# A Fourier-plus-experts kernel: the second group's key matrix gets its own space, five staged blocks move behind the first evictions, and token 512's row is normalized later

## The chip, the cores and the metric

The kernel runs on one core of a Trainium2 chip. The metric is device time in microseconds (us) from launch to the end of the program, and lower is better. Five engines work side by side, each through its own queue in order: TensorE (PE: matmuls, with PEld for its weight loads), VectorE (DVE), ScalarE (ACT), GpSimd (POOL) and SyncE (SP), whose queue issues nearly all the DMAs. An engine that reaches an instruction whose inputs are not there stands still, with everything behind it.

## The reference

The input `x` has 2048 tokens of 512 numbers. The output is the sum of three things:

```
xn = layernorm(x)
A  = C_seq.re @ (xn @ C_hid.re.T) - C_seq.im @ (xn @ C_hid.im.T)   # real part of a 2-D DFT
q  = xn @ w_q                       # 32 heads, two halves of 128
s1, s2 = q1 @ k1.T, q2 @ k2.T       # 64 first keys, 64 second keys
two best of each -> two best of the four pairs -> experts e, gates g = softmax
B  = sum over heads and experts of g * gelu(xn . u[e]) * v[e]
out = x + A + B
```

## The kernel before, in words

All the work that the change touches lies in the first tenth of the run. A planner (the framework's scheduler) simulates the program with its own costs and writes a fixed order for each engine's queue; where two instructions are ready in its simulation, the one earlier in the program goes first. The author steers it by adding dependencies that compute nothing: a column of zeros in the tile `zs` is made from a late result (`scale=0.0`) and given as `bias` to instructions that shall not be queued before that result.

**Normalization and folds.** The tokens lie in four groups g of four blocks of 128 (`x[q, g]`), handled in the order `G = (1, 0, 2, 3)`. `ln(g, n)` (from L335) takes the means and variances, for some blocks on ACT and for the rest on DVE, and then scales the four blocks in place: on ACT (L379), or on DVE through `norm` (L313), which before is used only for the first group (`n == 0`) and its blocks 0 and 2. `fold(k, g)` (L402 to L413) adds (k = 0) or subtracts (k = 1, "difference") mirrored rows and columns on DVE, through the tiles `ft`, `ff`, `fo` into `Q[k][g]`; with that the DFT over the sequence needs a quarter of the matmuls. `main(k, g)` (L433) multiplies `Q[k][g]` by a quarter of the DFT matrix, `A[k, g]`, which `load(k, g)` (L320) brought in as a tile `c`; the sums over g build up in four PSUM banks `p`. `evict(k)` (L499 to L503) copies these four banks to SBUF on ACT (L494, L497), and they are the same four banks that the next user of the tag `pa` needs: `main(1, 0)` after `evict(0)`. `spread()` (L423) makes a correction column `s5c` that half of `evict(0)` adds.

**Token 512's row.** One token that has no mirror image, `x5` (a single partition of 2 x 512), is normalized on ACT (L576), and then folded by `fold_row(0)` and `fold_row(1)` on POOL (L415 to L419, and L390 to L400 with POOL as the engine).

**Staged blocks.** `stage(i)` (L507 to L514) splits a normalized block into two 16-bit parts, a high part on ACT (L512) and the difference on DVE (L513), in one of eight staging places (the table `SB`, L505), and a transposing DMA on SP (L514) writes it to `xt[i]`, the operand of the score matmuls. Sixteen blocks are staged, the n-th of them being `TO[n]`. A staging place is used again by a later block only after the transposing DMA has read it.

**Keys.** Heads are handled in eight groups j of four. `m_mul(j, t, ...)` multiplies the query weights by the keys on PE (L142), and `m_parts(j)` (L224 to L229) splits the four resulting banks into two 16-bit parts: the high one on ACT (L227), the difference on DVE (L228). The result `m` is the moving operand of the score matmuls `s_mm` (L253), 12 for each block. For j = 0 and 2, 4, 6 it lies in the pool `MP[0]`; for odd j in `MP[1]`, which before is opened after `stA.close()` (L677), in the space that the tiles of the pool `da` leave.

**Early scores.** `early(n)` (L278) computes the first group's scores for the n-th staged block ahead of time and parks them in SBUF (L285): before, four of them at the first group's stage, n = 4 and 5 in front of `main(1, 1)`, n = 6 and 7 in front of `main(1, 3)`. Then `m_mul(1)` and `main(1, 3)` follow, and after them on PE the scores of n = 8 to 15. `sides()` (L457) and `sums`, `hid` (L516) finish single rows and columns of the DFT. In `part_b`, `scores` finds the two best keys of each head on DVE (MAX8, L862; FIND_INDEX8, L866). A copy of a corner of `m1` into the place of the best values (L922) holds that row of instructions back until the second keys are split.

**The rest of the run** computes scores for the other groups, then the experts' matmuls (`u_part` L997, `g_mm` L1035, `v_part` L1080); none of it is edited, except for where some single rows are kept.

**Buffers.** The tiles `raw` (4 KB a partition each) hold eight DFT quarters and the four tiles of the first query weights; ten of them exist before. `cst` is a pool that lives through the whole kernel.

Of the kernel before, what the change touches and what calls it, by code (L numbers as in the profile page):

```python
# [7 lines left out]
F32 = mybir.dt.float32  # L8
# [10 lines left out]
P = 128  # L19
# [15 lines left out]
def tile_fnet_peer(ctx, tc, x, ca, cb, c5, wt, wf, wr, wq, kt, ut, vn, out):  # L35
# [90 lines left out]
    MP = {}  # L126
# [128 lines left out]
                n += 1  # L255


    MP[0] = stS.enter_context(tc.tile_pool(name="mp0", bufs=1, side="left"))
    stE = ctx.enter_context(ExitStack())
    uvp = stE.enter_context(tc.tile_pool(name="uvp", bufs=1, side="right"))  # L260
    cmp_p = stE.enter_context(tc.tile_pool(name="cmpp", bufs=1, side="right"))
# [29 lines left out]
        xp[h] = da.tile([P, 2, 512], F32, name=f"x{h}")  # L291

    def raw_tile(name):
        return da.tile([P, 2, 512], F32, tag="raw", name=name, bufs=10)

    G = (1, 0, 2, 3)
    GK = G, (0, 1, 2, 3)
# [33 lines left out]
    zs = da.tile([P, 3], F32, name="zs")  # L331

    def ln(g, n):


        onact = {1: (0, 1), 3: (0,)}.get(n, ())
        for q in onact:
            junk = Q[1][g].rearrange("p a d -> p (a d)").bitcast(BF16)[:, 2:514]
            zero = 0.0
            if n == 3:  # L340

                zero = nm0[:, 0, 0:1]
                nc.scalar.activation(zero, xn(G[1], 3)[:, 0:1], AF.Copy, scale=0.0)
            nc.scalar.activation(junk, xn(g, q), AF.Identity, bias=zero, scale=1.0 / 512, accum_out=mvs[:, g, q, 0:1])
            nc.scalar.activation(junk, xn(g, q), AF.Square, bias=mvs[:, g, q, 0:1], scale=-1.0,
                                 accum_out=mvs[:, g, q, 1:2])
        if onact:
            v = mvs[:, g, 0:len(onact), 1]
            nc.scalar.activation(v, v, AF.Copy, scale=1.0 / 512)
        for q in range(4):  # L350
            if q in onact:
                continue
            if n == 0:
                st = da.tile([P, 6], F32, tag="st", name=f"st{g}_{q}", bufs=2)
            else:
# [11 lines left out]
        nc.vector.scalar_tensor_tensor(negm[:, g], mvs[:, g, :, 0], -1.0, rstd[:, g], op0=ALU.mult, op1=ALU.mult)  # L367
        if g == 0:
            nc.vector.tensor_scalar(nm0[:, 0], negm[:, 0, 2:4], not0, None, op0=ALU.mult)
            nc.vector.tensor_scalar(nm0[:, 1], rstd[:, 0, 2:4], not0, None, op0=ALU.mult)  # L370
        for q in (0, 2, 1, 3):
            t = xn(g, q)
            b, r = negm[:, g, q:q + 1], rstd[:, g, q:q + 1]
            if g == 0 and q > 1:
                b, r = nm0[:, 0, q - 2:q - 1], nm0[:, 1, q - 2:q - 1]
            if n == 0 and q % 2 == 0:
                norm(t, t, 4 * g + q)
            else:
                nc.scalar.activation(t, t, AF.Identity, bias=b, scale=r)  # L379
# [100 lines left out]
        nc.vector.tensor_tensor(a5[0:1, 0], a5[0:1, 0], r[:, 1, 0:257], op=ALU.add)  # L480

    PT = {}
    p256 = uf[12][:, 0:16].rearrange("p (n a) -> p n a", n=8)
    p5 = uf[13][:, 257:263]
    q5 = uf[13][0:1, 0:2]
    s256, a256 = [uf[i].rearrange("p (h t) -> p h t", h=2) for i in (0, 2)]
    a5 = uf[1][:, 0:514].rearrange("p (k d) -> p k d", k=2)

# [18 lines left out]
    def stage(i):  # L507

        src = xn(i // 4, i % 4)
        n = TO.index(i)  # L510
        t = u_sb[SB[n] // 2][:, SB[n] % 2].rearrange("p a k n -> p a (k n)")
        nc.scalar.activation(t[:, 0], src, AF.Identity, bias=zs[:, int(n > 3):int(n > 3) + 1])  # L512
        nc.vector.tensor_tensor(t[:, 1], src, t[:, 0], op=ALU.subtract)  # L513
        nc.sync.dma_start_transpose(xt[i].rearrange("p a k n -> p (a k) n"), t.rearrange("p a d -> p (a d)"))  # L514

# [30 lines left out]
    row512(0, c5r, nc.scalar)  # L546
    nc.gpsimd.tensor_copy(c52, c5r[:, 0:2])
    nc.scalar.dma_start(c55, cb[0, 0, 0, 0:1, 8, 0:1])
    for g in GK[1][:2]:
        load(1, g)  # L550
    wfs = uf[14][:, 0:512]
    for t in range(2):
        m_mul(0, t, (0, 1))
    for n, g in enumerate(G):
# [16 lines left out]
        if n == 1:  # L571
            nc.scalar.activation(zs[:, 0:1], xn(g, 3)[:, 0:1], AF.Copy, scale=0.0)
            for q in range(4):
                stage(4 * G[0] + q)
            for q in range(2):
                nc.scalar.activation(x5[:, q], x5[:, q], AF.Identity, bias=negm[0:1, 0, q + 2:q + 3],  # L576
                                     scale=rstd[0:1, 0, q + 2:q + 3])
            for h in GK[1][2:]:
                load(1, h)
            nc.sync.dma_start(wfs, wf)  # L580
            nc.sync.dma_start(w2, wr[:, 0:2].to_broadcast([P, 2]))
            row512(1, A[1, 0][0:1, 512:1024])
            m_load(1, lambda t: wq_view(t, w4), range(4))
        if n == 3:
            nc.scalar.activation(zs[:, 1:2], rstd[:, G[3], 0:1], AF.Copy, scale=0.0)
            fold_row(0)
            fold_row(1)
            for q in range(2):
                stage(q)
# [14 lines left out]
    for g in GK[1]:  # L604
        fold(1, g)
        if g == 0:
            nc.vector.tensor_copy(Q[1][0][0:1, 0, 1:256], s5i[:, 1:256])
            nc.scalar.activation(xp[1][0:1], x5, AF.Copy)
            for q in range(2, 4):
                stage(q)  # L610
        if g % 2:
            for b in range(3 + g, 5 + g):
                early(b)
        if g == 3:
            for t in range(4):
                m_low(1, t, s5c[:, 0, 0:1])
            for t in range(4):
                m_mul(1, t, range(KD))
        main(1, g)
        if g == 1:  # L620
            for t in range(4):
                m_prep(1, t, whp, s5c[:, 0, 0:1])
# [2 lines left out]
    sides()  # L625
    for q in range(4):
        stage(12 + q)
    evict(1)

    BS = {}  # L630
# [24 lines left out]
    def y_rows(n):  # L655

        if n == 8:
            hid(uf[13][0:1, 264:778], 1, [p5[:, dt:dt + 1] for dt in range(2)], q5,
                [p5[:, 3 + dt:4 + dt] for dt in range(2)], pc("hy5"))
            return  # L660
        g, q = divmod(n, 2)
# [3 lines left out]

    def y_store(n):
        if n == 8:
            t, a, b, r = uf[13][0:1, 264:778], y_d[2][0:1], y_d[3][0:1], slice(0, 1)
        else:
            g, q = divmod(n, 2)  # L670
            r = slice(0 if g else 1, P)
# [3 lines left out]
        nc.sync.dma_start(b[:, 256:512], t[r, 0:256])  # L675

    stA.close()  # L677
    MP[1] = stS.enter_context(tc.tile_pool(name="mp1", bufs=1, side="left"))

# [3 lines left out]
    def part_b(safe, stS, stP, stE, xt, u_sb, cmp_p, w4):  # L683
# [226 lines left out]
        for j in range(NCH):  # L910
# [613 lines left out]
```

## Time and profile before

| | |
|---|---|
| median of the runs, us | 1160.09 (1159.86 to 1160.1, 3 runs) |
| profiled execution, its own time, us | 1157.52 |
| span of that execution in the trace, us | 1155.7 |
| mean granted TensorE clock | 0.993 |
| PE busy | 1128.8 us, 98% of the span |
| DVE busy | 935.7 us, 81% |
| ACT busy | 606.8 us, 53% |
| POOL busy | 223.9 us, 19% |

The span is what the trace covers of the profiled execution; its time has 1.8 us more, around the span. In a timeline, a row gives the start, the length, the engine, the line of the kernel, the operation, the tile written and the tiles read, the shapes, and the number of instructions merged into it; in brackets stands how long the engine had been idle before, and what released it. Matmul ends are modelled, so a long "busy" PE can hide a slow clock; the granted clock of a stretch stands in the view by windows. A transfer's row shows only when SP issued it.

### The profile page before, as it was taken

Reading aid. Unit: us, or ns where it says so; the run is one execution under the profiler, and the core shown is the slowest. Engines: PE = TensorE matmul, PEld = TensorE weight load, DVE = VectorE, ACT = ScalarE, POOL = GpSimd, SP = SyncE. Lnnn points to the kernel's source line nnn. Section 1 sums busy time; section 2 is a strip of 40 time slices with the busy share of each in tenths; the row PEclk is TensorE's granted clock in tenths of the full one; section 3 lists DMA queues with packets and bytes.
Section 4 is the critical chain, followed back from the end, with each engine's and each line's share of the span. In section 5 each row is a group of like instructions: output and inputs, shape, how many; then the busy total and the mean of one; then the engine's idle time right before and its main releaser. Section 6 shows DMA issues by size and latency. Waiting matters only on the chain.

```text
span 1155.7 us, 25202 instructions
## 1 busy us (share of the span) xinstructions
PE 1128.8 (98%) x9866; PEld 719.0 (62%) x9866; DVE 935.7 (81%) x2853; ACT 606.8 (53%) x1045; POOL 223.9 (19%) x216
## 2 busy tenths in 40 slices
PE   5899999999999999999999999999999999999997
PEld 4345555445445459778478478469569559658763
DVE  7879989799898999974995894897886886788670
ACT  6645787687786635353445435535535435334440
POOL 3001474865865410000000000010010000000000
PEclk9999999999999999999999999999999999999999
DMA  9774265143241204261742743743545555452423
GB/s 339 211 201 155 70 205 181 61 160 128 74 165 46 83 15 123 90 210 38 246 158 98 237 160 104 220 165 135 185 159 174 169 173 168 156 166 66 134 77 104
DMA packets 98334, 167.81 MB, mean 145 GB/s; under 512 B 32916, under 2 KB 48155, under 8 KB 98206
## 3 DMA queue, kind: packets, MB, share of 16 engines
q1 hardware_dynamic: 97904, 166.04, 44.5%
q8 instruction: 79, 1.29, 0.5%
q14 instruction: 49, 0.40, 0.1%
q10 hardware_dynamic: 302, 0.08, 0.0%
HBM read 142.69 MB, written 17.63 MB: 139 GB/s over the span
## 4 chain that ended last, share of the span: by engine, by line
PE 89%; DVE 8%; ACT 1%; DMA 1%; issue 0%; DVEq 0%; ACTq 0%
PE z L997 29%; PE v L1080 28%; PE s L253 25%; PE g L1035 4%; PE m L142 2%; DVE u L862 1%; PE p L442 1%; DVE u L866 1%; DVE u L513 1%; DVE ft L409 1%; DVE sums L358 0%; DVE m L228 0%; DVE L L1025 0%; DMA xq<-u 0%; DVE ff L390 0%; DMA x<-in_x_dram 0%
## 5 line engine op out<-in xcount | busy, mean ns | idle before, releaser
L997 PE MATMUL z<-xb,u 128*128 128x256 f16 (+1 forms) x3840 | 342.6, 251 | 0.0
L997 PEld LDWEIGHTS <-u 128*128 128x128 f16 x3840 | 309.7, 98 | 26.4
L253 PE MATMUL s<-m,xq 128*128 128x512 f16 x1344 | 297.6, 379 | 0.0
L1080 PE MATMUL v<-v,act 128*128 128x512 f16 x1056 | 233.2, 379 | 0.0
L253 PEld LDWEIGHTS <-xq 128*128 128x128 f16 x1344 | 129.6, 98 | 151.2 <-issue 1.9
L1025 DVE TENSOR_TENSOR L<-io_lam,cmp 128x2048 f16<-128x2048 f16 x128 | 157.3, 1229 | 60.0 <-PE g L1035 60.0
L1080 PEld LDWEIGHTS <-act 128*128 128x128 f16 x1056 | 101.3, 98 | 117.7
L1093 POOL TENSOR_TENSOR y<-y,xr 128x512 f32<-128x512 f32 x15 | 26.5, 1767 | 612.8 <-DMA y<-y_d 472.7
L862 DVE MAX8 vals<-ss 128x8 f32<-128x64 f32 x896 | 133.7, 216 | 2.6 <-ACT ss L858 2.5
L1004 ACT ACTIVATE act<-z,scl 128x256 f32<-128x256 f32 (+1 forms) x152 | 72.7, 502 | 120.1 <-PE z L997 120.1
L858 ACT ACTIVATE ss<-s,wsc 128x512 f32<-128x512 f32 x120 | 80.6, 682 | 56.3 <-PE s L253 45.7
L1080 PE MATMUL v<-v,w 128*128 128x512 f16 x480 | 106.2, 379 | 0.0
L1156 ACT ACTIVATE cx<-cx 128x896 f32<-128x896 f32 x64 | 60.5, 946 | 70.5 <-DVE cx L1136 52.0
L866 DVE FIND_INDEX8 idx<-vals,ss 128x8 uint16<-128x256 f32 x224 | 93.8, 419 | 0.0
L1050 ACT ACTIVATE act<-w 128x1024 f16<-128x1024 f32 x36 | 48.3, 1358 | 60.0 <-DVE w L1043 59.6
L1080 PEld LDWEIGHTS <-w 128*128 128x128 f16 x480 | 46.1, 98 | 53.3
L1043 DVE SCALAR_TENSOR_TENSOR w<-act,scl,g 128x1024 f32<-128x1024 f32 x44 | 55.7, 1276 | 19.8 <-ACT act L1004 19.8
L1130 DVE TENSOR_TENSOR cx<-cx 128x512 f32<-128x512 f32 (+2 forms) x84 | 48.4, 609 | 26.0 <-DMA cx<-in_cb_dram 24.7
L1035 PEld LDWEIGHTS <-L 128*128 128x128 f16 x2048 | 60.7, 96 | 11.3 <-DVE R L1033 1.3
L1035 PE MATMUL g<-R,L 128*128 128x32 f16 x2048 | 61.9, 176 | 0.3 <-DVE R L1033 0.2
L1033 DVE TENSOR_TENSOR R<-R,cmp 128x512 f16<-128x512 f16 x128 | 60.2, 470 | 1.5
L1004 ACT ACTIVATE w<-z,scl 128x256 f32<-128x256 f32 (+1 forms) x72 | 35.4, 492 | 49.3 <-PE z L997 49.3
(298 smaller groups left out, 1322.8 us busy)
## 6 DMA issues: line engine op xcount, KB each, us to landing
v<-v_d SPq DMA_DIRECT2D x67, 512.0 KB, 5.2
cx<-in_cb_dram SPq DMA_DIRECT2D x64, 448.0 KB, 5.2
w<-in_wq_dram SPq DMA_DIRECT2D x28, 512.0 KB, 5.9
fit<-in_wq_dram SPq DMA_DIRECT2D x28, 512.0 KB, 4.9
uv<-in_vn_dram SPq DMA_DIRECT2D x16, 512.0 KB, 3.8
uv<-in_ut_dram SPq DMA_DIRECT2D x16, 512.0 KB, 3.9
c<-in_ca_dram SPq DMA_DIRECT2D x8, 512.0 KB
y<-y_d SPq DMA_DIRECT2D x16, 256.0 KB, 2.7
```

The source lines that it names most:

```text
L253: nc.tensor.matmul(ps, xt[i][:, l, kd, :], m[:, r, kd, :], start=(n == 0), stop=(n == 3 * KD - 1))
L858: nc.scalar.activation(s, ps, AF.Copy, scale=inv)
L862: nc.vector.max(vals[:, i, w, :, h], s[:, g, :])
L866: nc.vector.max_index(idx[:, i, w].rearrange("p k h -> p (k h)"), vals[:, i, w, 0:2].rearrange("p k h -> p (k h)"), s[:, w * HC:g + 1, :]. ...
L997: nc.tensor.matmul(ps if n == 1 else ps.rearrange("p (b n) -> p b n", b=2), ug[:, l, c % 2, kd, :], xb2[:, k0, r, kd, :] if n == 1 else xb ...
L1004: nc.scalar.activation(ACT[bb][:, cg * m:cg * m + m, :], pv[:, i], AF.Gelu_apprx_tanh, scale=zsc)
L1025: nc.vector.tensor_tensor(L.rearrange("p t (l two) -> p t l two", two=2), io_lam.rearrange("p (l two) -> p l two", two=2).unsqueeze(1).to_ ...
L1033: nc.vector.tensor_tensor(Rv, Rv, bc(2, NC), op=ALU.mult)
L1035: nc.tensor.matmul(p[:, hf, t * NC:(t + 1) * NC], L[:, t, :], R[:, t, :], start=True, stop=True)
L1043: nc.vector.scalar_tensor_tensor(w, act[:, :, ts], fw, p.rearrange("p h (n c) -> p c (h n)", c=NC), op0=ALU.mult, op1=ALU.mult)
L1080: nc.tensor.matmul(pv, w16[:, c, :, l], v_sb[g][:, r, cc, :], start=(n + cc == 0 and k == 0), stop=(n == 15 and cc == 1 and k == 2))
L1156: later.append(lambda: nc.scalar.activation(tf[:, P:], tf[:, P:], AF.Abs, accum_out=chk[:, n:n + 1]))
```

## The change

- **Second keys.** `MP[1]` is opened beside `MP[0]`, ahead of the pool `da`, so that it has space of its own. The tiles `raw` go from ten to eight. The split `m_stage(1, ..., 5)` and `(..., 6)`, which is `m_parts(1)`, is called in front of `main(1, 3)` and no longer at the beginning of `part_b`.
- **Loads.** `load(1, 0)` and `load(1, 1)`, which were issued with the first loads, are issued with the other two after the first group's staging.
- **Staged blocks.** The zero column that blocks n = 11 to 15 take as bias is `zs[:, 2]`, made after `evict(0)` (L601); before, they took `zs[:, 1]`.
- **Token 512.** The two normalizing instructions of `x5` move from step n = 1 to step n = 2 and take their bias from a new tile `nm5`, which hangs on a new zero column made from group 2's normalized rows.
- **Normalization.** `norm` on DVE is used for blocks 0 and 2 of the last group too (`n in (0, 3)`).
- **Early scores.** n = 6 and 7 are computed after `sides()` and the last staging, in front of `evict(1)`.
- **Places.** `p256`, `p5` and `q5` get a small tile in `cst`, and `y5` moves from `uf[13]` to `uf[5]`.

```diff
-    MP[0] = stS.enter_context(tc.tile_pool(name="mp0", bufs=1, side="left"))
+    for k in range(2):
+        MP[k] = stS.enter_context(tc.tile_pool(name=f"mp{k}", bufs=1, side="left"))
...
-        return da.tile([P, 2, 512], F32, tag="raw", name=name, bufs=10)
+        return da.tile([P, 2, 512], F32, tag="raw", name=name, bufs=8)
...
-            if n == 0 and q % 2 == 0:
+            if n in (0, 3) and q % 2 == 0:
                 norm(t, t, 4 * g + q)
...
-    p256 = uf[12][:, 0:16].rearrange("p (n a) -> p n a", n=8)
-    p5 = uf[13][:, 257:263]
-    q5 = uf[13][0:1, 0:2]
+    ps = cst.tile([P, 24], F32, name="ps")
+    y5 = uf[5][0:1, 0:514]
...
-        nc.scalar.activation(t[:, 0], src, AF.Identity, bias=zs[:, int(n > 3):int(n > 3) + 1])
+        nc.scalar.activation(t[:, 0], src, AF.Identity, bias=zs[:, (n > 3) + (n > 10):(n > 3) + (n > 10) + 1])
...
-    for g in GK[1][:2]:
-        load(1, g)
...
-            for q in range(2):
-                nc.scalar.activation(x5[:, q], x5[:, q], AF.Identity, bias=negm[0:1, 0, q + 2:q + 3],
-                                     scale=rstd[0:1, 0, q + 2:q + 3])
-            for h in GK[1][2:]:
+            for h in GK[1]:
                 load(1, h)
...
+        if n == 2:
+            nc.scalar.activation(zs[:, 3:4], xn(g, 3)[:, 0:1], AF.Copy, scale=0.0)
+            nc.scalar.activation(nm5, negm[0:1, 0, 2:4], AF.Identity, bias=zs[0:1, 3:4])
+            for q in range(2):
+                nc.scalar.activation(x5[:, q], x5[:, q], AF.Identity, bias=nm5[:, q:q + 1],
+                                     scale=rstd[0:1, 0, q + 2:q + 3])
...
-        if g % 2:
-            for b in range(3 + g, 5 + g):
+        if g == 1:
+            for b in range(4, 6):
                 early(b)
...
                 m_mul(1, t, range(KD))
+            for n in range(5, 7):
+                m_stage(1, None, n)
         main(1, g)
...
         stage(12 + q)
+    for b in range(6, 8):
+        early(b)
     evict(1)
...
-    MP[1] = stS.enter_context(tc.tile_pool(name="mp1", bufs=1, side="left"))
...
-                for n in range(5, 7):
-                    m_stage(1, wq_tile, n)
```

More of the change, by code (lines that the diff above doesn't have):

```diff
@@ L329, in tile_fnet_peer @@
     nm0 = da.tile([P, 2, 2], F32, name="nm0")
-    zs = da.tile([P, 3], F32, name="zs")
+    zs = da.tile([P, 4], F32, name="zs")
+    nm5 = da.tile([1, 2], F32, name="nm5")
     def ln(g, n):
@@ L482, in tile_fnet_peer @@
     PT = {}
-    p256 = uf[12][:, 0:16].rearrange("p (n a) -> p n a", n=8)
-    p5 = uf[13][:, 257:263]
-    q5 = uf[13][0:1, 0:2]
+    ps = cst.tile([P, 24], F32, name="ps")
+    y5 = uf[5][0:1, 0:514]
+    p256 = ps[:, 0:16].rearrange("p (n a) -> p n a", n=8)
+    p5 = ps[:, 16:22]
+    q5 = ps[0:1, 22:24]
     s256, a256 = [uf[i].rearrange("p (h t) -> p h t", h=2) for i in (0, 2)]
@@ L657, in y_rows @@
         if n == 8:
-            hid(uf[13][0:1, 264:778], 1, [p5[:, dt:dt + 1] for dt in range(2)], q5,
+            hid(y5, 1, [p5[:, dt:dt + 1] for dt in range(2)], q5,
                 [p5[:, 3 + dt:4 + dt] for dt in range(2)], pc("hy5"))
@@ L667, in y_store @@
         if n == 8:
-            t, a, b, r = uf[13][0:1, 264:778], y_d[2][0:1], y_d[3][0:1], slice(0, 1)
+            t, a, b, r = y5, y_d[2][0:1], y_d[3][0:1], slice(0, 1)
         else:
```

## The prediction

> **What bounds the kernel now.** I read the page first, then PE's waits over the whole run.
>
> ```profile
> span 1155.7 us, 25202 instructions
> PE 1128.8 (98%) x9866; PEld 719.0 (62%) x9866; DVE 935.7 (81%) x2853; ACT 606.8 (53%) x1045; POOL 223.9 (19%) x216
> PE m L146 <- DMA wq<-in_wq_dram: 9.3, 1, 9.3
> PE p L442 <- ACT u L494: 5.1, 1, 5.1
> PE p L442 <- DVE q L412: 4.1, 2, 3.9
> PE m L142 <- DVE uvpFalse L117: 1.2, 1, 1.2
> PE hy L518 <- DVE u L530: 0.5, 1, 0.5
> PE m L142 <- ACT u L285: 0.2, 1, 0.2
> 132.38 0.22 PE L142 MATMUL m<-sums,wh 128*128 128x64 f16 x2 [1.22 <-DVE uvpFalse L117]
> ```
>
> PE is idle for 1155.7 - 1128.8 = 26.9 us. 9.3 us of it lie ahead of the first matmul. The five other waits of the list make 11.1 us, and what is left of the 26.9 lies at the very end, where no matmul waits. The last row puts the latest wait of weight at 132; from there to the end PE always has work. So whatever PE gains in the first 132 us comes off the end, and nothing else does. The two large waits, in order of time:
>
> ```profile
> 28.87 5.59 PE L442 MATMUL p<-c,q 128*128 128x512 f32 x8 [3.87 <-DVE q L412]
> 44.65 3.60 PE L442 MATMUL p<-c,q 128*128 128x512 f32 x8
> 48.47 3.70 PE L442 MATMUL p<-c,q 128*128 128x512 f32 x8 [0.22 <-DVE q L412]
> 59.10 4.97 PE L442 MATMUL p<-c,q 128*128 128x512 f32 x6 [5.13 <-ACT u L494]
> 28.90:34.30 5.40, 5.40 (x9) 2.29 (x10) 5.40 (x9) 4.60 (x12) 1.41 (x2) 0.65 0.91 162
> 59.10:64.00 4.90, 4.90 (x7) 2.02 (x8) 4.90 (x10) 4.87 (x10) 0.00 (x0) 0.56 1.10 227
> ```
>
> Behind each of them PE runs slowly: the granted clock (third number from the end of the window rows) is 0.65 and 0.56, and a matmul piece takes about 4.97/7 = 0.71 us from 59.10 (six in the row and one merged elsewhere), against 3.60/8 = 0.45.
>
> **The change part by part.**
>
> *1. Five staged blocks behind evict(0).* ACT's queue around the second wait:
>
> ```profile
> 51.62 0.58 ACT L494 ACTIVATE u<-p 128x512 f32<-128x512 f32 x1
> 57.78 0.72 ACT L512 ACTIVATE u<-xq,zs 128x512 f16<-128x512 f32 x1 [5.58 <-DMA xq<-u]
> 58.46 0.59 ACT L494 ACTIVATE u<-p 128x512 f32<-128x512 f32 x1
> 58.94 1.59 ACT L497 ACTIVATE u<-p,s5c 128x256 f32<-128x256 f32 x4
> 53.26 1.24 SPq L514 DMA_TRANSPOSE xq<-u  x1
> ```
>
> One bank is evicted at 51.62. Then a staging instruction (L512) waits until 57.78 for a transposing DMA to empty its staging place, and three evictions stand behind it. The transpose it waits for was issued at 53.26. By the table of places, blocks n = 7 to 10 reuse places that the first group's transposes emptied long before, so the waiter is one of n = 12 to 14. The change puts n = 11 to 15 behind `zs[:, 2]`, which is made after evict(0). The next eviction then follows the first at 52.2. PE's next need, the second bank, is met at about 52.8, and the rest follow within about 1.6 us, in pace with matmuls of two pieces of 0.45 us. I leave 0.5 us of the 5.13: **-4.6**, bounds -5.1 (all) and -2 (something else in ACT's queue takes its place). With so short a wait the clock need not fall: 7 x (0.71 - 0.45) = **-1.8**, bounds 0 and -2.2 (4.90 us at 0.56).
>
> *2. Token 512 later; two normalizations on DVE.* These set when `Q[0][3]`, the last sum, reaches PE.
>
> ```profile
> 21.89 1.26 POOL L418 TENSOR_TENSOR r<-u 1x512 f32<-1x512 f32 x1 [8.49 <-ACT u L576]
> 29.42 0.89 POOL L400 TENSOR_TENSOR s5i<-r 1x127 f32<-1x127 f32 x1
> 21.96 1.74 DVE L390 TENSOR_TENSOR ff<-ft 128x508 f32<-128x508 f32 x1
> 36.74 0.67 DVE L390 TENSOR_TENSOR ff<-ft 128x508 f32<-128x508 f32 x1
> 26.29 1.75 DVE L513 TENSOR_TENSOR u<-x,u 128x512 f16<-128x512 f32 x1
> 44.31 0.68 DVE L513 TENSOR_TENSOR u<-x,u 128x512 f16<-128x512 f32 x1
> 36.25 0.21 ACT L398 ACTIVATE ff<-ft 128x4 f32<-128x4 f32 x1 [2.65 <-DVE ft L409]
> 39.44 0.16 DVE L367 SCALAR_TENSOR_TENSOR negm<-mvs,rstd 128x4 f32<-128x4 f32 x1
> 39.64 2.22 ACT L379 ACTIVATE xq<-xq,negm,rstd 128x512 f32<-128x512 f32 x3
> 43.17 1.23 DVE L409 TENSOR_TENSOR ft<-xq,xq 128x1024 f32<-128x1024 f32 x1 [3.57 <-ACT xq L379]
> 8.85 1.00 DVE L313 TENSOR_SCALAR x<-x,mvs,rstd 128x512 f32<-128x512 f32 x2
> ```
>
> From 21.89 to 30.31 POOL folds token 512, and the same DVE instructions take longer then than later: 1.74 against 0.67, 1.75 against 0.68. These two alone lose 2.1 us, just ahead of the 3.87 us wait. Once the row waits for group 2's normalization, POOL starts after this group is scaled, behind the chain to `Q[0][0]`, which is then 2.1 us shorter or, with the other instructions between, up to 3.9 (the wait itself). POOL's 8.4 us then meet the chain of `Q[0][2]` and `Q[0][3]` and may take from it anything between nothing and as much as before. ACT's two `x5` instructions move to where it waits 2.65 us for DVE; without that cover they would cost what they take. Normalizing the last group: DVE idles 3.57 us for four rows on ACT; with two on each engine it takes 1.00 us on DVE and two thirds of 2.22 on ACT, and `ft` starts about 1.7 us sooner. Sum for the start of `main(0, 3)` at 48.47: 1.7 alone if POOL takes it all back, 1.7 + 3.9 if it takes nothing: between -1.7 and -5.6. I take about the middle, **-3.5**. PE itself can be there that early: it loses the 3.87 and part of the slow 5.59 behind it.
>
> The Trainium skill has a rule that speaks against this part: SBUF — State Buffer, "Who interferes with whom", says that GpSimd reads through DVE's second port, and that a DVE instruction with two SBUF inputs and a GpSimd instruction that reads SBUF shut each other out for a whole instruction. The rows agree in kind (two-input instructions, lengthened by up to the length of POOL's own); by that rule the contention moves along with the row, which is rival A.
>
> *3. Second keys.* Where DVE stands today:
>
> ```profile
> 78.29 1.88 DVE L513 TENSOR_TENSOR u<-xq,u 128x512 f16<-128x512 f32 x3
> 88.91 2.48 DVE L228 SCALAR_TENSOR_TENSOR m<-m,m 128x512 f16<-128x512 f32 x4 [8.74 <-ACT m L227]
> 91.68 0.49 DVE L862 MAX8 u<-u 128x8 f32<-128x64 f32 x3
> 87.59 5.34 PE L253 MATMUL s<-m,xq 128*128 128x512 f16 x24
> 66.29 2.46 DVE L167 SCALAR_TENSOR_TENSOR w<-w,s5c,wh 128x1024 f16<-128x1024 f32 x2
> 80.92 0.22 PE L142 MATMUL m<-sums,wh 128*128 128x64 f16 x2
> 32.74 1.03 SPq L323 DMA_DIRECT2D c<-in_ca_dram  x2
> ```
>
> DVE is through with its backlog at 80.17 and idles 8.74 us, because the split needs the place that `da` leaves. With a home it comes behind `m_mul(1)`: the first MAX8 stands 91.68 - 88.91 = 2.77 us behind the split's first DVE row, so it then starts at 80.17 + 2.77 = 82.9, less the 3.5 of part 2: 79.4, 12.3 us sooner. PE starts on the scores of n = 8 at 87.59 less what it gains above, 9.9: 77.7. DVE is then 1.7 us behind PE there, where it is 91.68 - 87.59 = 4.1 behind today. The late waits on DVE and ACT (1.2 + 0.5 + 0.2) should shrink: **-1.0**, bounds 0 and -1.9. On the other side PE reaches `m_mul(1)`, with `early(6)` and `early(7)` gone from in front of it, at 80.92 - 5.3 (two blocks) - 9.9 = 65.7, and needs DVE's last `l` part (now 68.75, then 65.3); and the two early blocks need banks that the split must free first. **+0.5**, bounds 0 and +3.
>
> *4. At nothing.* The four `c` loads wait for places that PE's first key matmuls give back ahead of 28.87, and for SP's queue, where the first group's transposes stand; two are issued at 32.7 now, and in this queue all four then are. `c` of `main(1, 0)` is wanted at about 59.10 - 9.9 = 49. If that cover were gone, the wait would appear as PE on DMA. The places of `p256`, `p5` and `y5` only remove waits on ACT; the two new tiny ACT instructions (0.21 us as L398 above) lie in ACT's idle time.
>
> **Sum.** -3.5 - 4.6 - 1.8 - 1.0 + 0.5 = -10.4 on the profiled execution's own 1157.52 (span 1155.7 and 1.8 around it): 1147.1. The median of the runs shown is 2.6 above that execution, so 1160.09 - 10.4 = **1149.7**. Ends: -5.6 - 5.1 - 2.2 - 1.9 = -14.8, and -1.7 - 2 - 0 - 0 + 3 = -0.7.
>
> **The rivals.**
>
> *A. POOL's contention moves along in full.* POOL's row then costs `Q[0][3]` what it spared `Q[0][0]`: part 2 gives -1.7, the sum is -8.6, **1151.5**. For it: DVE between 31 and 40 runs the same kind of two-input instructions. Against: DVE idles 3.57 us there.
>
> *B. DVE becomes the bound before the scores.* From 43.17 to 80.17 no row of DVE's timeline has idle time in front of it, and this queue starts only 3.5 us or less earlier and gets 2.8 us more. If its planned order puts the split or the late staging ahead of the `l` parts, PE stands at `m_mul(1)` for 4 to 5 us more: -6, **1154**.
>
> *C. The change doesn't open the eviction*, since some other instruction with a late input stands in front of it in ACT's new order. Only part 2 stays: -3.5, **1156.6**.
>
> *D. Slower: the last staged blocks come too late.*
>
> ```profile
> L862 DVE MAX8 vals<-ss 128x8 f32<-128x64 f32 x896 | 133.7, 216 | 2.6 <-ACT ss L858 2.5
> L866 DVE FIND_INDEX8 idx<-vals,ss 128x8 uint16<-128x256 f32 x224 | 93.8, 419 | 0.0
> ```
>
> Their subtractions (L513) now can fall behind the MAX8 rows, which may start at 79.4. Eight early blocks at (133.7 + 93.8)/112 = 2.0 us make 16; the first subtraction would run at 95.6 and its transpose land 5 us later (53.26 to 57.7 above, and 0.7), at 100.7, where PE, three blocks of 2.7 us after n = 8, wants n = 11 at 77.7 + 8 = 85.7 or, with the single rows between, 87. PE would stand about 13.7 us: +3.3, **1163.4**. It decides from six blocks on. Against: today the last three subtractions stand ahead of MAX8, at 78.29, as in the program.
>
> **How the numbers follow.** Forecast 0.50 (its own range 1147 to 1151.3), A 0.16, B 0.19, C 0.07, D 0.08. The 80% range is 1146 to 1156: it takes in A and B and most of the good ends, and leaves out C and D. A difference of 0.2% (2.3 us) is about what a measurement of this kernel can tell from none; C lies near it, and I split it. Faster 0.88, same 0.04, slower 0.08.
>
> **What would show it.** Right: L494 and L497 in one run on ACT with no L512 wait among them; PE's wait on ACT u L494 under 1 us, and the granted clock behind it near 1; L390 and L513 on DVE back near 0.67 before 30 us; no long DVE wait for ACT m L227. Wrong: a new PE wait at `m_mul(1)` on DVE w L167 (B), L412 or L413 long between 32 and 45 (A), PE scores waiting on a transposing DMA (D), or the old 5 us wait with another name (C).

## The result

Four runs of the changed kernel gave a median of 1152.91 us (1151.37 to 1153.35), beside 1159.97 (1159.31 to 1160.1) for four runs of the kernel before: a ratio of 0.9938, 95% interval 0.9921 to 0.9955, so 7.06 us less. The forecast was 10.4 less, 1149.7; the time lies inside the range and above the forecast's own part of it. Which kernels come out where is in the table ahead of the experiments; here is the profile after.

One line of the page, and PE's four longest waits over the whole run (us in total, times, longest):

```profile
span 1151.1 us, 25211 instructions
```

```profile
PE m L146 <- DMA wq<-in_wq_dram: 9.5, 1, 9.5
PE m L142 <- DVE uvpFalse L117: 3.4, 1, 3.4
PE p L444 <- DVE q L414: 3.3, 1, 3.3
PE hy L522 <- DVE u L534: 1.0, 1, 1.0
```

The 5.1 us wait for the evictions is gone, and so is the 3.9 us wait ahead of `main(0, 0)`. But one wait for `Q` of 3.3 us is there (now ahead of `main(0, 3)`), and the late wait for L117 has grown from 1.2 to 3.4. PE's timeline shows where its lead comes and goes (L444 is the old L442; the rows of before are in the prediction, and more of them stand below):

```profile
26.06 3.65 PE L444 MATMUL p<-c,q 128*128 128x512 f32 x8
...
46.76 3.70 PE L444 MATMUL p<-c,q 128*128 128x512 f32 x8 [3.26 <-DVE q L414]
...
50.92 3.70 PE L444 MATMUL p<-c,q 128*128 128x512 f32 x8
54.46 5.34 PE L253 MATMUL s<-m,xb 128*128 128x512 f16 x24
...
72.83 10.52 PE L253 MATMUL s<-m,xq 128*128 128x512 f16 x48
...
114.86 0.28 PE L116 MATMUL uvs<-asums,ones 128*128 128x2 f32 x2
115.00 2.75 PE L253 MATMUL s<-m,xq 128*128 128x512 f16 x12
...
118.51 0.60 PE L253 MATMUL s<-m,xq 128*128 128x512 f16 x2
122.49 0.22 PE L142 MATMUL m<-sums,wh 128*128 128x64 f16 x2 [3.38 <-DVE uvpFalse L117]
...
146.68 0.39 PE L522 MATMUL hy<-u,u 128*128 128x129 f32 x2
```

From before's timeline, the rows around the wait for the evictions, the stretch at the sum for `uv_scale` (L116), and the same matmul of the second group's single rows:

```profile
52.63 1.13 PE L442 MATMUL p<-c,q 128*128 128x512 f32 x2
53.59 0.38 PE L253 MATMUL s<-m,xb 128*128 128x512 f16 x1
...
63.91 5.13 PE L253 MATMUL s<-m,xb 128*128 128x512 f16 x23
...
123.99 0.28 PE L116 MATMUL uvs<-asums,ones 128*128 128x2 f32 x2
124.13 2.75 PE L253 MATMUL s<-m,xq 128*128 128x512 f16 x12
127.07 2.11 PE L253 MATMUL s<-m,xq 128*128 128x512 f16 x9
129.19 0.81 PE L253 MATMUL s<-m,xq 128*128 128x512 f16 x3
130.36 0.81 PE L253 MATMUL s<-m,xq 128*128 128x512 f16 x3
...
151.61 0.39 PE L518 MATMUL hy<-u,u 128*128 128x129 f32 x2
```

Put side by side, PE's lead over before is:

| place | before | after | lead, us |
|---|---|---|---|
| `main(0, 0)` | 28.87 | 26.06 | 2.8 |
| `main(0, 3)` | 48.47 | 46.76 | 1.7 |
| early scores ahead of `main(1, 1)` (before: the first of the 24 had run at 53.59) | 63.91 | 54.46 | 9.5 |
| scores of n = 8 (after: the last 24 of the 48 from 72.83, so 72.83 + 10.52/2) | 87.59 | 78.1 | 9.5 |
| sum for `uv_scale`, L116 | 123.99 | 114.86 | 9.1 |
| single rows of the second group | 151.61 | 146.68 | 4.9 |
| span | 1155.7 | 1151.1 | 4.6 |

Up to 78 us the change gives nearly the sum that was forecast (9.5 where 9.9 was expected), though not from the same parts. Between 115 and 147 half of it is lost. Behind the sum, PE has only 12 + 2 score matmuls to do before the planner's order sends it to a key matmul that needs a PSUM bank; before, it had 12 + 9 + 3 + 3 = 27. There are two banks of this tag (`pc`), and `uvs` holds one until L117 on DVE has read it. DVE and ACT around these places:

```profile
22.55 0.68 DVE L392 TENSOR_TENSOR ff<-ft 128x508 f32<-128x508 f32 x1
...
34.16 1.47 DVE L392 TENSOR_TENSOR ff<-ft 128x508 f32<-128x508 f32 x1
...
38.50 1.12 DVE L369 SCALAR_TENSOR_TENSOR negm<-mvs,rstd 128x4 f32<-128x4 f32 x1
...
78.99 1.88 DVE L517 TENSOR_TENSOR u<-xq,u 128x512 f16<-128x512 f32 x3
81.04 0.74 DVE L870 MAX8 u<-u 128x8 f32<-128x64 f32 x5
...
122.30 0.14 DVE L117 TENSOR_SCALAR uvpFalse<-uvs 128x2 f32<-128x2 f32 x1
```

```profile
49.64 0.60 ACT L498 ACTIVATE u<-p 128x512 f32<-128x512 f32 x1 [0.82 <-PE p L444]
50.50 0.60 ACT L498 ACTIVATE u<-p 128x512 f32<-128x512 f32 x1 [0.26 <-PE p L444]
...
51.24 1.61 ACT L501 ACTIVATE u<-p,s5c 128x256 f32<-128x256 f32 x4
```

L117 takes 0.14 us and starts 7.4 us after its matmul, because DVE takes it in its place behind rows of MAX8, FIND_INDEX8 and single rows, and a CAST of 1.91 us (L816). The windows after show what the wait does to the clock (the third number from the end):

```profile
122.60:126.00 3.40, 3.40 (x19) 1.43 (x18) 2.70 (x19) 0.00 (x0) 2.64 (x10) 0.67 0.26 96
126.00:130.00 4.00, 4.00 (x46) 2.58 (x45) 3.82 (x24) 0.74 (x2) 0.42 (x2) 0.86 0.08 28
```

Waiting costs 3.4 us here, where it cost 1.2 before; the slow clock costs 3.40 x 0.33 + 4.00 x 0.14 = 1.7 more, and a wait of 0.24 us at 118.34, not in the list above, is new. That is 2.4 + 1.7, or 4.1 of the 4.2 us that go between 114.86 and 146.68.

### The profile page after: what moved, and what is told of

Its sections match the earlier page's. It is cut to its first block, busy times and chain, and to the rows that moved or that the text cites. A ratio compares the mean times of both kernels' runs of the same rounds, so it can differ in the third digit from the quotient of the medians.

```text
span 1151.1 us, 25211 instructions
## 1 busy us (share of the span) xinstructions
PE 1127.1 (98%) x9866; PEld 718.9 (62%) x9866; DVE 936.6 (81%) x2855; ACT 605.8 (53%) x1045; POOL 225.3 (20%) x216
## 4 chain that ended last, share of the span: by engine, by line
PE 64%; DVE 23%; POOL 5%; ACT 3%; issue 3%; DMA 2%; SPq 0%; POOLq 0%; DVEq 0%; ACTq 0%
PE v L1086 28%; PE z L1003 26%; DVE vals L870 5%; DVE idx L874 5%; PE s L253 4%; PE g L1041 4%; POOL w L162 2%; DVE m L228 1%; DVE u L870 1%; DVE L L1031 1%; PE m L146 1%; POOL w L163 1%; DVE z L812 1%; DVE u L874 1%; DVE z L811 1%
## 5 line engine op out<-in xcount | busy, mean ns | idle before, releaser
L1057 DVE TENSOR_TENSOR act<-w,act 128x1024 f16<-128x1024 f32 x44 | 59.0, 1343 | 3.7 <-ACT act L1056 3.7
```

The lines of the kernel that those rows point to most:

```text
L1057: nc.vector.tensor_tensor(w16[..., 1], w, w16[..., 0], op=ALU.subtract)
```

## The experiments

The theories. **Theory 1:** the gain up to 78 us is the opened eviction, which the staging edit brings by itself, and of part 2 little is left, since POOL's contention moved along with the row (rival A of the prediction). Its rivals: the row and the normalization carry the gain, or all edits add up. **Theory 2:** what is lost between 115 and 147 is the PSUM bank that `uvs` holds, so that with the sum elsewhere the whole lead reaches the end. Its rival: DVE's backlog, which began earlier, costs PE the same at another place.

Each kernel was timed beside the kernel before on the same chip; before's median there was 1158.56 to 1158.8. Kernels of different rows are compared by their ratios.

| kernel | median, us | ratio to before, 95% | span, us |
|---|---|---|---|
| the change | 1152.91 | 0.9938 (0.9921 to 0.9955) | 1151.1 |
| staging edit alone | 1150.22 | 0.9928 (0.9915 to 0.9941) | 1149.1 |
| token 512's row alone | 1152.11 | 0.9943 (0.993 to 0.9955) | 1149.6 |
| normalization alone | 1155.15 | 0.9969 (0.9958 to 0.998) | 1154.4 |
| change without the staging edit | 1151.86 | 0.9946 (0.9933 to 0.9959) | 1150.3 |
| staging, normalization, row one step earlier | 1150.54 | 0.9925 (0.991 to 0.9939) | 1149.2 |
| change, sum two places earlier | 1150.23 | 0.9927 (0.9915 to 0.994) | 1150.1 |
| **change, sum in another bank** | **1147.45** | 0.9906 (0.9891 to 0.992) | 1144.8 |
| staging edit, sum in another bank | 1149.23 | 0.9921 (0.9907 to 0.9934) | 1147.1 |
| change without the home | 1153.27 | 0.9956 (0.9943 to 0.9969) | 1150.1 |
| the same, sum in another bank | 1150.11 | 0.9922 (0.9909 to 0.9936) | 1147.5 |
| change, sum in another bank, POOL's folds left out | 1144.96 | 0.9879 (0.9864 to 0.9895) | 1143.5 |
| change, sum in another bank, blocks tied to `Q[0][3]` | 1147.6 | 0.9906 (0.9891 to 0.9921) | 1145.8 |

### Which part opens the eviction

**The staging edit alone**, on the kernel before:

```diff
-        nc.scalar.activation(t[:, 0], src, AF.Identity, bias=zs[:, int(n > 3):int(n > 3) + 1])
+        nc.scalar.activation(t[:, 0], src, AF.Identity, bias=zs[:, (n > 3) + (n > 10):(n > 3) + (n > 10) + 1])
```

> The kernel before with one edit: blocks n = 11 to 15 take the zero column made after evict(0). Theory 1 (the eviction): PE's 5.1 us wait on ACT u L494 goes and the clock behind it stays up, 5 to 7.5 us less than before, about 1153.5; PE's position at the scores of n = 8 is 6 to 8 us earlier, less what the waits at 118 to 132 give back. Rival (the folds on DVE are the real gate): 0 to 2 us less, with PE waiting for Q[1] or for the l parts instead.

PE's waits and one row of its timeline:

```profile
PE p L442 <- DVE q L412: 3.8, 1, 3.8
PE m L142 <- DVE uvpFalse L117: 1.2, 1, 1.2
```

```profile
52.76 3.70 PE L442 MATMUL p<-c,q 128*128 128x512 f32 x8
```

The wait for the evictions is gone, the one for `Q[0][0]` stays, and `main(1, 0)` runs through at 3.70 us for 8 where it took 4.97 for 6. 0.72% is 8.3 us (6.8 to 9.8 by the interval): a single line brings as much as the whole change, as far as the intervals tell. In its trace PE's lead is 7.4 us, at the scores of n = 8 (80.19) as well as at the second group's single rows (144.22), inside the 5 to 7.5 expected. Theory 1 holds for this part.

**Token 512's row alone**, on the kernel before (the two `x5` instructions at n == 2, with `nm5` and its zero column):

```diff
-            for q in range(2):
-                nc.scalar.activation(x5[:, q], x5[:, q], AF.Identity, bias=negm[0:1, 0, q + 2:q + 3],
-                                     scale=rstd[0:1, 0, q + 2:q + 3])
...
+        if n == 2:
+            nc.scalar.activation(zs[:, 3:4], xn(g, 3)[:, 0:1], AF.Copy, scale=0.0)
+            nc.scalar.activation(nm5, negm[0:1, 0, 2:4], AF.Identity, bias=zs[0:1, 3:4])
```

> The kernel before with one edit: token 512's row is normalized at step n = 2. Theory 1 (POOL's contention moves along with the row): main(0,0) starts 3 to 4 us earlier, main(0,3) within 0.7 us of before, and the time is within 1 us of before, about 1160. Rival (the contention is spared): main(0,3) starts 2 to 4 us earlier and the time is 2 to 4 us less.

PE's timeline, and then ACT's:

```profile
26.04 3.70 PE L443 MATMUL p<-c,q 128*128 128x512 f32 x8
...
48.21 5.35 PE L443 MATMUL p<-c,q 128*128 128x512 f32 x8 [4.67 <-DVE q L413]
```

```profile
54.33 1.60 ACT L498 ACTIVATE u<-p,s5c 128x256 f32<-128x256 f32 x4
...
57.59 0.72 ACT L513 ACTIVATE u<-xq,zs 128x512 f16<-128x512 f32 x1 [1.58 <-DMA xq<-u]
```

At the sums it went nearly as expected: `main(0, 0)` starts 2.8 us sooner (28.87 to 26.04; 3 to 4 were expected) and `main(0, 3)` only 0.26 (48.47 to 48.21), so POOL takes back what it spared. Yet the kernel gained 6.6 us (0.57%), where about none was expected. The second fence tells why: the waiting staging instruction now stands behind the four evictions, without the edit that was meant to put it there. The planner's order had changed with the row. This is a miss for theory 1, which held the staging edit to be the only key.

**The normalization alone**, on the kernel before:

```diff
-            if n == 0 and q % 2 == 0:
+            if n in (0, 3) and q % 2 == 0:
```

> The kernel before with one edit: blocks 0 and 2 of the last group are normalized on DVE. Theory (the 5 us wait depends on where ACT's planned order puts block n = 12's staging; here it stands ahead of both evictions): the wait on the evictions stays or grows, main(0,3) starts no later than before, and the time is within 1.5 us of before. Rival (any edit of the fold chain frees the evictions): 5 us less or better.

```profile
54.25 0.72 ACT L512 ACTIVATE u<-xq,zs 128x512 f16<-128x512 f32 x1 [3.97 <-DMA xq<-u]
54.88 1.06 ACT L494 ACTIVATE u<-p 128x512 f32<-128x512 f32 x2
```

In ACT's queue the staging instruction still stands ahead of the evictions, now ahead of both, and PE waits 2.3 us there, not 5.1: the bound, an emptied staging place, comes at 54.25 and no longer at 57.78. I had expected the wait to stay or grow and the time to move by less than 1.5 us; the wait fell to less than half, and the time by 0.31% or 3.6 us.

**The change without the staging edit:**

```diff
-bias=zs[:, (n > 3) + (n > 10):(n > 3) + (n > 10) + 1])
+bias=zs[:, int(n > 3):int(n > 3) + 1])
```

> The changed kernel with one edit undone: blocks n = 11 to 15 take the zero column of before. Theory 1: the 5 us wait on L498 and the slow clock come back, 5 to 7 us more than the changed kernel, 1158 to 1160. Rival: 0 to 2 us more, since the other edits carry the gain.

A second miss in the same direction: the wait doesn't come back. The evictions start at 50.44 and 51.74, right behind their matmuls, and the time moves from 0.9938 to 0.9946, well inside the intervals.

**Staging and normalization, with the row tied to group 2's statistics instead of its normalized blocks**, on the kernel before (no home for the second keys):

```diff
+        if n == 1:
+            nc.scalar.activation(zs[:, 3:4], negm[:, G[2], 3:4], AF.Copy, scale=0.0)
```

> The kernel before with three edits: blocks n = 11 to 15 staged behind evict(0), the last group's blocks 0 and 2 normalized on DVE, and token 512's row behind the negated means of group 2 (not behind its scaled rows, so POOL folds it between the two chains on DVE). No home for the second keys. Theory: both PE waits on the sums Q (3.9 at 25, and 3.3 at 43 in the changed kernel) shrink below 1.5 us each, PE reaches the scores of n = 8 9 to 11 us sooner than before, and the time is 8.5 to 11 us less than before. Rival (POOL's contention just finds the next chain): PE still waits 3 us on Q, and the time is 6.5 to 8.5 us less, as with the staging edit alone.

The row was meant to fall between the two chains. The planner put the `x5` instructions at 29.97 on ACT, so POOL began at 31.55, only 2.3 us sooner than in the changed kernel (33.81), and `main(0, 3)` still waits 3.4 us for `Q`, with a granted clock of 0.68 behind it. The time is 0.75% or 8.7 us less than before, at the edge between theory and rival. So this doesn't say whether a place between the chains would help.

What follows from the five: before's 5.1 us wait was an accident of one planned order, in which a block that had to wait for a DMA stood between two evictions. The staging edit rules that order out. The row did so as well by a new plan, and the normalization shortened it. Alone they bring 8.3, 6.6 and 3.6 us, 18.5 together, where the whole change brings 7.1: they pay for the same wait. (The 7.1 has lost some 4 us at another place, which comes next; without that loss the whole change brings 10.9, still far from 18.5.)

### Where the rest was lost

**The sum two places earlier** in the list of work between the scores, on the changed kernel:

```diff
-            todo[18].append(lambda at: uv_scale())
+            todo[16].append(lambda at: uv_scale())
```

> The changed kernel with uv_scale two blocks of scores earlier (its bank is read by DVE well before the key matmuls of j = 2 need the bank). Theory 2 (the 3.4 us wait of PE on DVE uvpFalse L117 and the slow clock behind it ate 4 us of the gain): about 4 us less than the changed kernel, 1149. Rival (DVE's backlog is the bound there, and PE would wait as long at the next bank): within 1 us of the changed kernel, 1152 to 1153.5, with another PE wait of 3 us between 105 and 135.

```profile
PE uvs L116 <- DVE u L534: 1.5, 1, 1.5
PE g L1041 <- DVE R L1039: 1.1, 3, 0.5
```

The wait of 3.4 is gone, but now the sum itself waits 1.5 us for a bank that DVE's single rows (L534) hold, and later rows wait more. The gain is about 1.3 us (0.9938 to 0.9927, inside the intervals) where 4 was expected. Moving the sum within the two banks only moves the wait to the next holder of a bank, as theory 2's rival has it, though the wait there is 1.5 us and not 3.

**The sum in the other pool**, tag `pa`, whose four banks are free at that time:

```diff
-            p, q = pow2(mx, wqp, f"uvp{safe}", 2, None if safe else pc("uvs"))
+            p, q = pow2(mx, wqp, f"uvp{safe}", 2, None if safe else pa("uvs"))
```

> The changed kernel with the sum for uv_scale in one of the four score banks and not in one of the two banks that the key matmuls of j = 2 need. Theory (the 3.4 us bank wait and the slow clock behind it ate the gain): no PE wait on uvpFalse, 3 to 5 us less than the changed kernel. Rival (DVE's backlog is the bound there): within 1 us of the changed kernel, with PE waiting 2 us or more for another bank between 105 and 135.

PE's waits and the second group's first single row:

```profile
PE p L444 <- DVE q L414: 3.0, 1, 3.0
PE hy L522 <- DVE u L534: 0.9, 1, 0.9
PE g L1041 <- DVE R L1039: 0.2, 1, 0.2
```

```profile
140.97 0.39 PE L522 MATMUL hy<-u,u 128*128 128x129 f32 x2
```

The wait behind the sum is gone and no other has grown in its place. The lead at 140.97 is 10.6 us (151.61 before), and the span is 10.9 us shorter. DVE reads the sum as late as ever (L117 at 121.95, 7.5 us after its matmul at 114.49): only the bank was missing. The ratio of 0.9906 is 0.32% or 3.7 us below the change, inside the 3 to 5 expected, and the two intervals just don't overlap. Theory 2 holds, and this version beats both kernels.

**The staging edit with the sum in the other pool**, on the kernel before, both diffs as above:

> Before with two edits alone: blocks 11 to 15 staged behind the first evictions, and the sum for uv_scale in a bank of the other PSUM pool. Theory (row, normalization and home are worth little by themselves, and what they are worth reaches the end only when the bank is free): the wait of 1.2 us behind the sum goes, the wait of 3.8 us ahead of main(0,0) stays, and the time is 1 to 1.5 us below that of the staging edit alone, so about 9.5 us below before, 1149.3, and 1.5 to 2 us above the changed kernel with the sum moved. Rival (those three edits are worth nothing): as fast as the changed kernel with the sum moved, about 11 us below before.

1149.23 us, 9.2 below before and, by the ratios, 0.8 below the staging edit alone; the 1.2 us wait is gone, and 2.6 us stay ahead of `main(0, 0)`. Against the change with the sum moved it is 0.15% or 1.7 us slower. Both differences lie within the intervals, but the traces agree with them: the 48 score matmuls ahead of the second group's single rows start at 133.85 with the staging edit alone, at 132.34 here and at 130.61 in the change with the sum moved. That is about the theory's size: the rest of the change (row, normalization, home and the smaller edits together) is worth some 2 us, and only when the bank is free; with the bank in the way, the change starts these matmuls at 136.32, behind the staging edit alone.

### What the home of the second keys is worth

**The change without it:** `MP[1]` is opened behind `stA.close()` again and the split is called in `part_b`.

```diff
-    for k in range(2):
-        MP[k] = stS.enter_context(tc.tile_pool(name=f"mp{k}", bufs=1, side="left"))
+    MP[0] = stS.enter_context(tc.tile_pool(name="mp0", bufs=1, side="left"))
...
-            for n in range(5, 7):
-                m_stage(1, None, n)
...
     stA.close()
+    MP[1] = stS.enter_context(tc.tile_pool(name="mp1", bufs=1, side="left"))
```

> The changed kernel with one edit undone: the second keys lie again in the place that the pool da leaves and are split at the beginning of part_b. Theory (the home closes an 8.7 us idle stretch of DVE, but 2.5 us of splitting come in instead and DVE's other backlog fills the rest): the first MAX8 starts 1 to 2 us later than in the changed kernel, and the time is 0 to 2 us more than the changed kernel. Rival (the home is worth what it closes): 4 us more or worse, with a DVE idle of 5 us or more in front of the split.

```profile
78.15 6.63 PE L253 MATMUL s<-m,xq 128*128 128x512 f16 x30 [2.25 <-DVE m L228]
```

It is 0.18% or 2 us slower by the ratios, with overlapping intervals, and its trace shows no loss: the span is 1.0 us shorter than the change's. The first MAX8 is at 80.19, earlier than with the home (81.04), not later: the place comes free sooner by itself, since PE is done with `da`'s tiles sooner (`main(1, 3)` starts at 68.34, where before it was 84.07). What the home spares is PE's wait for the split, 2.25 us. Without it, other waits are shorter: 1.4 us in place of 3.3 for `Q`, 2.5 in place of 3.4 behind the sum, and none for `hy`, where the change has 1.0. So these two kernels don't show that the home is worth anything while the bank is held.

The wait of 2.5 behind the sum also says where PE's short order comes from. Between L116 and the key matmul PE has 12 + 3 score matmuls here, without the home, and 12 + 2 without the staging edit. With the staging edit, the row or the normalization alone, and with the three of them together (the row one step earlier), it still has 27, and the wait is 1.2. So the order comes from the edits that are left, the loads, the early scores and the places, or from several together; no run separates them.

**The same with the sum in the other pool:**

> The changed kernel with the sum for uv_scale moved, but without the second keys' home (pool opened after da is closed, split in part_b). Theory (the home is worth what DVE's head start is worth at the sums, single rows and scores, not only at the bank): 1.5 to 2 us slower than the changed kernel with the sum moved, with PE waiting for the split (m L228) or for hy. Rival (the home only helps by way of the bank): within 0.5 us of it, no wait of PE over 1 us behind 60.

```profile
78.34 8.26 PE L253 MATMUL s<-m,xq 128*128 128x512 f16 x30 [2.25 <-DVE m L228]
```

0.9922 against 0.9906: 1.9 us slower than with the home, the theory's 1.5 to 2 (the intervals overlap). The trace has the place: 2.25 us of waiting for the split, and behind it 30 matmuls in 8.26 us, 0.275 each, where the 48 at 72.83 in the change took 10.52, 0.219 each; the granted clock from 78.30 to 81.70 is 0.51. In the kernel above, the same wait of 2.25 us had a full clock behind it. So with the bank free the home is worth about 2 us, through PE's wait and not through the bank, and part of these 2 us is a slow clock that need not follow.

### What is left ahead of `main(0, 3)`

**Without POOL's folds.** On the kernel with the sum moved; this one leaves out the folds of token 512, and zeros stand in for their results:

```diff
-        r = da.tile([1, 1, 1024], F32, tag="r5", name=f"r5_{k}", bufs=1)
-        nc.gpsimd.tensor_tensor(r[:, 0, 0:512], x5[:, 0], x5[:, 1], op=ALU.subtract if k else ALU.add)
-        fold_d(k, r[:, :, 0:512], r[:, :, 512:768], (s5i if k else s5).unsqueeze(1), nc.gpsimd)
+        nc.gpsimd.memset(s5i if k else s5, 0.0)
```

> The changed kernel with the sum moved; POOL's fold of token 512 (11 instructions, 8.4 us) is left out and its two results are set to zero. Theory (DVE pays for POOL's work wherever it lies, and that is why moving the row gave main(0,3) only 1.7 us): DVE's rows between 33.8 and 43 are as short as elsewhere (L392 0.67, L369 0.16), the wait of 3.0 us ahead of main(0,3) falls to below 0.7, and the time falls by 2 to 3 us. Rival (the chain to the last sum is bound by ACT's normalization or by the order of DVE's queue, not by POOL): the wait stays above 2 and the time falls by less than 1 us.

DVE's timeline:

```profile
32.70 0.67 DVE L392 TENSOR_TENSOR ff<-ft 128x508 f32<-128x508 f32 x1
...
35.92 0.16 DVE L369 SCALAR_TENSOR_TENSOR negm<-mvs,rstd 128x4 f32<-128x4 f32 x1
...
38.52 1.23 DVE L411 TENSOR_TENSOR ft<-xq,xq 128x1024 f32<-128x1024 f32 x1 [1.53 <-ACT xq L381]
```

L392 is back from 1.46 to 0.67 and L369 from 1.11 to 0.16 (the kernel with the sum moved has 1.46 and 1.11). The last group's `ft` starts at 38.52 where it stood at 40.86, and the last sum (the L414 row behind it) at 43.35 where it stood at 45.94. PE no longer waits ahead of `main(0, 3)`, and the time falls by 2.5 us in the medians and 3.1 by the ratios (the intervals overlap by a hair), as the theory had it. So POOL's work costs the chain to the last sum 2.6 us, and moving the row had only moved this price. A wait of 1.1 us ahead of `main(0, 0)` is new in this kernel: PE's first key matmuls start 1.1 us sooner (21.08, and 22.21 with the folds) while `Q[0][0]` comes when it came. That wait costs nothing by itself, but the granted clock behind it is 0.67, and the eight pieces take 5.36 us and not 3.70.

**Two subtractions out of the chain:** the blocks n = 4 to 10 hang on the last sum instead of the last group's statistics.

```diff
-            nc.scalar.activation(zs[:, 1:2], rstd[:, G[3], 0:1], AF.Copy, scale=0.0)
+            nc.scalar.activation(zs[:, 1:2], Q[0][g][:, 1, 0:1], AF.Copy, scale=0.0)
```

> The changed kernel with the sum moved; the zero column of the staged blocks 4 to 10 is made from the last sum Q[0][3] and no longer from the last group's statistics, so that the two subtractions of 0.94 and 0.68 us that stand inside the chain to this sum come behind it. Theory (what is left of the wait ahead of main(0,3) is DVE's own queue): the wait of 3.0 falls to about 1.4 and the time falls by about 1.5 us. Rival (the blocks now come too late): PE waits 1 to 2 us for a transposing DMA ahead of early block 4, or for the evictions behind the new high parts, and the time stays or rises.

PE's timeline and ACT's:

```profile
45.23 3.70 PE L444 MATMUL p<-c,q 128*128 128x512 f32 x8 [1.66 <-DVE q L414]
...
51.04 5.40 PE L444 MATMUL p<-c,q 128*128 128x512 f32 x8 [1.58 <-ACT u L498]
```

```profile
47.35 3.16 ACT L516 ACTIVATE u<-xq,zs 128x512 f16<-128x512 f32 x5
```

Theory and rival both came true: the wait for the last sum falls from 3.0 to 1.66, and the high parts, all due at once now, stand ahead of the evictions for 3.16 us, so that PE waits 1.58 there and has a slow clock (0.68) behind it. The time is the same (0.9906 both times).

## Why the prediction was right or wrong

**Part 1, the eviction: the mechanism right, the size short.** The evictions run in one stretch with no L516 between them, as the prediction asked for. Between `main(1, 0)` and the early scores behind it PE took 63.91 - 52.63 = 11.3 us before and takes 54.46 - 50.92 = 3.5 now. That is 7.7 where 4.6 + 1.8 was put down. All of the 5.13 wait went, where 0.5 of it was left standing. The slow clock cost 2.2 rather than 1.8: the prediction counted seven pieces behind 59.10, but the seventh matmul of its window is the first score matmul at 63.91. Six pieces took 63.91 - 59.10 = 4.8 us, 0.80 each, and now take 0.44 each (3.54/8). The 0.4 that remains is mostly the score matmul that before had run ahead of the wait (at 53.59). What the prediction didn't see is that the row edit alone would have opened the eviction too; it costed the edits as if each had a wait of its own.

**Part 2, -3.5: failed, at "I take about the middle".** The step gave 1.7, the bound at which "POOL takes it all back". L392 is 0.68 at 22.55 as predicted, and the same line is 1.47 at 34.16. The kernel without the folds shows that this is POOL: 2.6 us on the way to the last sum. The rule of the Trainium skill that the prediction quoted against this part (SBUF — State Buffer, "Who interferes with whom") was the better guide (the last section has the trace's rows for it), and rival A named the mechanism. The argument against A, DVE's 3.57 us of idle time, failed because that time lies behind the delayed rows. DVE idles there for ACT's normalization, which needs the negated means of L369, and POOL's delays fall on L369 and ahead of it. L369 ends at 38.50 + 1.12 = 39.62 after the change; before, the same line (then L367) ended at 39.44 + 0.16 = 39.60, so by there nothing is left of the 2.8 us won at `main(0, 0)`; without the folds it ends at 36.08. The 1.7 that came are the normalization's: `ft` starts at 41.21 and no longer at 43.17, with 0.35 us of idle time left ahead of it.

**Part 3, "the late waits should shrink: -1.0": failed.** They grew, from 1.2 + 0.5 + 0.2 to 3.4 + 1.0 + 0.2, with a slow clock of 1.7 us behind the first. The step took a wait of PE on DVE for a sign of DVE's lag, and the lag in fact shrank: L117 came 8.2 us after its matmul before (123.99 to 132.2) and 7.4 after. What decided was how much work PE's planned order put in between, for one of two banks: 7.2 us before and 4.0 after, since 13 score matmuls at 0.22 us and a few key matmuls now come later. That is 3.2 less, and with the 0.8 by which L117 came sooner 2.4 are left; the wait grew by 2.2, and the new one of 0.24 comes on top. The kernel with another bank shows that nothing else was missing. Which edit shortened the order stays open among the loads, the early scores, the places and several edits together. The home's own share was misread too: the first MAX8 comes 10.6 us sooner, close to the 12.3 put down, but it does so without the home as well.

**Rivals.** A's mechanism happened, though its sum of -8.6 didn't: it had the same late step. B and D didn't: no wait at `m_mul(1)`, and the last three subtractions (78.99) stand ahead of the first MAX8 (81.04). C didn't. Part 4 was right: PE waits for no DMA after the first weights.

**The sum.** 1.7 + 7.7 = 9.4 of lead, against 9.9; 4.9 of the 9.5 at the scores of n = 8 given back, against 0.5 of further gain: 4.6 in the spans, and 7.1 in the medians. The 2.5 between these two numbers is the distance between before's profiled execution (1157.52) and its median; after's profile lies on its median (1152.88 and 1152.91). The prediction carried that distance over as if it belonged to the kernel. The other timings of before run from 1156.81 to 1160.16, so an execution of 1157.52 is nothing special; there is no trace of a longer one, and what those 2.5 us were stays open. That the lead at the scores came out so close to its sum is luck: part 2 brought 1.8 less than its term and part 1 brought 1.3 more.

## What to carry to other kernels

When several edits aim at waits close to each other, ask for each whether another one removes the same wait: alone three of these brought 18.5 us, and the whole change 7.1, or 10.9 once the late bank was free. A lead won early has to pass every later place where a small buffer is held by a short instruction in a long queue, so count, for each late wait, the work that the planned order puts between the writer and the next user of that buffer, before calling it smaller. And contention between two engines doesn't vanish by moving the work of one in time if the delayed instructions stand in the chain at the new place too; idle time of the other engine behind them doesn't take it up.

## What the runs showed of the hardware

**Even a tiny DVE instruction can be held until a POOL instruction ends.** POOL's timeline after:

```profile
33.81 1.27 POOL L420 TENSOR_TENSOR r<-u 1x512 f32<-1x512 f32 x1 [20.12 <-ACT u L587]
...
38.33 1.27 POOL L420 TENSOR_TENSOR r<-u 1x512 f32<-1x512 f32 x1
```

The 4-element L369 ends at 38.50 + 1.12 = 39.62, with POOL's row at 38.33 + 1.27 = 39.60; without the folds it takes 0.16. So a POOL instruction on a single partition can hold up a DVE instruction on 128.

**How long PE waits doesn't settle whether its clock falls.** After 3.26 us at 46.76 the eight pieces took 3.70; after 1.58 us in the last experiment they took 5.40. The two kernels without the home show it with equal waits: 2.25 us at 78.15 and 2.25 us at 78.34, and the granted clock behind them was 1.00 (78.10 to 81.70) in the one and 0.51 (78.30 to 81.70) in the other. The Trainium skill ("TensorE: Matmul & The Clock Gate", "What's actually happening") gives a free-running window of about 3.4 us and a slow clock after at least one idle window. That the phase matters would fit the 3.26 and the pair of equal waits; a slow clock behind a wait of 1.58 doesn't fit a whole idle window, and no run here shows what else decided.
